# adaLN attention and gMLP block: first norm's modulation summed on TensorE, w_qkv read in column halves

## The chip, the cores and the metric

One core of one Trainium2 chip runs the kernel. The metric is the device time in microseconds of one execution, as the median of several runs. Five engines take part: TensorE (PE; its weight loads are PEld), VectorE (DVE), ScalarE (ACT), GpSimd (POOL) and SyncE (SP), which issues nearly all DMAs.

## The reference

All data is float32, S = 2048 rows, D = 448 columns, 16 heads of 28.

```python
x = A_x
mod = (silu(c) @ w_mod).reshape(1, 6, 1, 448)
sa, ca, ga, sb, cb, gb = mod[:, 0], ..., mod[:, 5]
h = layernorm(x) * (1 + ca) + sa
q, k, v = split(h @ wqkv)                 # 448 -> 3 x 448, 16 heads of 28
o = softmax(q @ k.T * 28**-0.5) @ v
x = x + ga * (o @ wo)
h = layernorm(x) * (1 + cb) + sb
z = gelu(h @ w_in)                        # 448 -> 1792
g = w_sp @ layernorm(z[..., 896:]) + b_sp # mixes the 2048 rows
x = x + gb * ((z[..., :896] * g) @ w_out)
```

## The kernel before

The stages come one after the other: projections of the first norm (about the first 95 us, with the rest of q and k up to 165 us), attention head by head, the output projection, the gMLP's two input projections, the row mixing and the output. The change is in the projections.

**Numbers.** A product keeps float32 accuracy by splitting each factor into a rounded high part and the remaining low part (`hi`, `lo`; `sub` computes `lo = value - hi`, line 83) and adding up the products. `STEPS` lists the 11 pairs (part of hT, part of the weight) that make one product over the 448 rows of a weight; 448 is three chunks of 128 and one of 64, and the low part of the last chunk lies in the upper half of its tile. So one V tile (128 rows of x, `v_tiles`, line 271) and one q/k unit (128 columns of w_qkv by 512 rows, `qk_unit(m, g)`, line 280) are 11 matmuls each. The columns of q and k are seven blocks m = 0 to 6; head 0 needs blocks 0 and 3.

**Groups.** The 2048 rows of x are four groups g of four tiles. For each group: `load_x`; `ln_stats` (VectorE's statistics, then `rstd_of`, two small POOL instructions, lines 106 and 107); `ln_norm` (VectorE's four `xn` tiles, line 253; POOL copies the last 64 columns once more behind them, line 263); `ln_transpose` (TensorE's 16 transposes into four PSUM tiles, line 116; then for chunks c = 0, 2, 1, 3 the scale and shift by the columns `ca` and `sa`, the rounding to hi, and lo). For groups 1 to 3 scale and rounding are ScalarE's (lines 123 and 130) and lo is POOL's. Group 0 shares them out between ScalarE with POOL and VectorE.

**Modulation.** `w_mod` is read in three pairs (sa with ca, ga with sb, cb with gb), each as four tiles of 112 rows. `mod_acc(pair, k)` adds `silu[k] * wm` on VectorE (lines 214 and 216). `mod_col` turns a summed row into per-partition columns by matmuls with ones (line 222); `mod_bc` broadcasts a row to all partitions by a matmul (line 230). Pair 0 is summed ahead of the first transposes' use, pair 1 at the end of group 1 and pair 2 at the end of group 2; `ga` and `sb` are made at the end of group 2's V tiles, `cb` and `gb` after group 3.

**Weights.** `load_w` reads w_qkv by row chunks: the V part (448 columns) and, into the same four buffers (tag `raw`), the q/k part of 896 columns. ScalarE makes the high parts (`wv_hi` line 297, `weight_part` line 94); POOL makes V's low parts, and POOL and VectorE alternate for q and k.

**Order.** The schedule is written by hand: every engine executes its instructions in the order in which the program issues them, and so does SP with its DMAs. PSUM has a ring of seven tiles (`bank`) and one more (`ps_o`). In each group the order on TensorE is: V tiles, the next group's transposes, the other V tiles, q/k units 0 and 3. `pe_fill` runs matmuls whose result nobody reads. After group 3, units (m, g) for m = 4, 1, 5, 2, 6 and all g follow; between their steps `m_first` computes the first 80 score products for the row maxima (line 399), each followed by a reduction on VectorE (line 404). They read q and k of the first heads, which go through DRAM (`qk_scr`, line 288) and come back by `load_head`.

Of the kernel before, what the change touches and what calls it, by code (L numbers as in the profile page):

```python
# [8 lines left out]
F32 = mybir.dt.float32  # L9
# [24 lines left out]
def tile_adaln_mha_gmlp(ctx, tc, x, wqkv, wo, w_in, w_spT, b_sp, w_out, cT, w_mod, out):  # L34
# [47 lines left out]
    def sub(eng, dst, a, hi):  # L82
        eng.tensor_tensor(out=dst, in0=a, in1=hi.bitcast(F32), op=ALU.subtract)  # L83
# [2 lines left out]
        eng.dma_start(dst[0:64], src)  # L86
        eng.dma_start(dst[64:128], src)

    def weight_part(dst, i, raw, hi_eng, lo_eng, zero=True):

        n = raw.shape[-1]
        h = dst[:, i if i < 3 else 6, 0:n]
        if hi_eng is act:
            act.activation(h, raw, AF.Copy)
        else:
            hi_eng.tensor_copy(h, raw)
        if i < 3:
            sub(lo_eng, dst[:, 3 + i, 0:n], raw, h)
        else:
            sub(lo_eng, dst[0:64, 7, 0:n], raw[0:64], h[0:64])  # L100
            if zero:
                pool.memset(dst[64:128, 7, 0:n].bitcast(F32), 0.0)

    def rstd_of(var, rs, n):

# [55 lines left out]
    def bank(name):  # L161
        return ring.tile([128, 512], F32, name=name, tag="s")

    def load_mod(pair, eng):
        for k in range(4):
            wms[pair, k] = e1.tile([112, 2, D], F32, name="wm", bufs=4)
            eng.dma_start(wms[pair, k], w_mod[:, pair, k])

    def load_x(g, eng):
# [3 lines left out]
        for t in range(4):  # L173
            xts[4 * g + t] = xg[:, t, :]

    def load_w(kind, i, eng):
        c0, n = (2 * D, D) if kind == "v" else (0, 2 * D)
        raw = e1.tile([128, 2 * D], F32, name="raw", bufs=4)[:, :n]
# [4 lines left out]
        raws[kind, i] = raw  # L183

    cc_t = e1.tile([112, 4], F32, name="cc_t", bufs=1)
    sp.dma_start(cc_t, cT)
# [13 lines left out]

    wu = bank("wu")

    def pe_fill(n):
        for _ in range(n):
            pe.matmul(wu[:, 0:128], ones, ones, start=True, stop=True)

    accs = {}

# [6 lines left out]
        else:  # L215
            dve.scalar_tensor_tensor(out=acc, in0=wm, scalar=silu[:, k : k + 1], in1=acc, op0=ALU.mult, op1=ALU.add)

    def mod_col(*parts):
        pc = bank("pc")
        for i, (nm, acc, plus1) in enumerate(parts):  # L220
            for c, r, e in ((0, 0, 128), (1, 0, 128), (2, 0, 128), (3, 0, 64), (3, 64, 128)):
                pe.matmul(
                    pc[r:e, 4 * i + c : 4 * i + c + 1], acc[:, c * 128 : c * 128 + e - r], ones[:112, 0:1], start=True, stop=True
                )
        for i, (nm, acc, plus1) in enumerate(parts):
            dve.tensor_scalar(out=cols[nm], in0=pc[:, 4 * i : 4 * i + 4], scalar1=plus1, scalar2=None, op0=ALU.add)

    def mod_bc(nm, acc):
        pc = bank("pc")
# [18 lines left out]
    def ln_norm(g):  # L248
        mv, rs = mv1.pop(g)
        res = []  # L250
        for t in range(4):
            xn = e1.tile([128, 512], F32, name="xn", bufs=4)
            dve.tensor_scalar(
                out=xn[:, :D],
                in0=xts.pop(4 * g + t),
                scalar1=mv[:, t, 0:1],
                scalar2=rs[:, t : t + 1],
                op0=ALU.subtract,
                op1=ALU.mult,
            )  # L260
# [5 lines left out]
    def v_tiles(*kts):  # L266
        pvs = [bank("pv") for _ in kts]
        for j, (a, b) in enumerate(STEPS):
            for kt, pv in zip(kts, pvs):
                g, t = divmod(kt, 4)  # L270
                pe.matmul(pv[:, :D], hT[g][:, a, t * 128 : (t + 1) * 128], wv[:, b, :], start=j == 0, stop=j == NST - 1)  # L271
        for kt, pv in zip(kts, pvs):
            dve.tensor_copy(V[:, kt, :, 0:DH], pv[:, :D].rearrange("p (h d) -> p h d", d=DH))

    def qk_unit(m, g, mid=None):
        pq = bank("pq")
        for j, (a, b) in enumerate(STEPS):
            if mid and j in mid:
                mid[j]()
            pe.matmul(pq, wqk[:, b, m * 128 : (m + 1) * 128], hT[g][:, a, :], start=j == 0, stop=j == NST - 1)  # L280
        f = stage.tile([128, 512], F32, name="qf")
        act.activation(f, pq, AF.Copy)  # L282
        hi = stage.tile([128, 512], F32R, name="qh")
        act.activation(hi, f, AF.Copy)
        lo = stage2.tile([128, 512], F32R, name="ql")
        sub(pool, lo, f, hi)
        for i, t in enumerate((hi, lo)):
            sp.dma_start(qk_scr[i][m * 128 : (m + 1) * 128, g * 512 : (g + 1) * 512], t.bitcast(F32))

    ln_stats(0)  # L290
    mod_acc(0, 0)
    mod_acc(0, 1)
    xns = ln_norm(0)
    mod_acc(0, 2)
    mod_acc(0, 3)
    def wv_hi(i):
        act.activation(wv[:, i if i < 3 else 6, :], raws["v", i], AF.Copy)

    def wv_lo(i):
# [3 lines left out]
        else:  # L303
            sub(pool, wv[0:64, 7, :], raw[0:64], wv[0:64, 6, :])

    for i in (0, 2):
        wv_hi(i)
        wv_lo(i)

    def wv_rest(c):  # L310
        if c == 2:
            wv_hi(1)
            wv_lo(1)
        if c == 1:
            wv_hi(3)
            wv_lo(3)

    def mod_first():
        pe_fill(4)
        mod_col(("ca", accs[0][:, 1, :], 1.0), ("sa", accs[0][:, 0, :], 0.0))  # L320
        pe_fill(10)

    ln_transpose(
        xns, e1, hT[0], cols["ca"], cols["sa"], (act, act, dve, dve), (pool, pool, dve, dve), mod_first, wv_rest
    )
    load_x(1, sp)
    for i in range(4):
        load_w("qk", i, sp)
    ln_stats(1)
    xns = ln_norm(1)  # L330
    for g in range(NG):
        if g + 2 < NG:
            load_x(g + 2, sp)
        if g in (0, 2):
            load_mod(1 + g // 2, sp)
        if g == 3:
            early.close()
            stk = att.enter_context(tc.tile_pool(name="stk", bufs=1))
            kq = [[stk.tile([128, S], F32R, name=f"{n}st{i}") for n in "kq"] for i in range(3)]
            kst, qst = [a[0] for a in kq], [a[1] for a in kq]  # L340
            npool = att.enter_context(tc.tile_pool(name="npool", bufs=2))

            def load_head(h, c0=0, c1=S):
                k, q = kst[h % 3], qst[h % 3]
                if h < 2 and c0 == 0:
                    pool.memset(k[64:86, :].bitcast(F32), 1.0)
                for r0, i in ((0, 0), (56, 1), (28, 0)):
                    sp.dma_start(k[r0 : r0 + 28, c0:c1].bitcast(F32), qk_scr[i][D + h * DH : D + (h + 1) * DH, c0:c1])
                for r0, i in ((0, 0), (28, 1), (56, 0)):
                    sp.dma_start(q[r0 : r0 + 28, c0:c1].bitcast(F32), qk_scr[i][h * DH : (h + 1) * DH, c0:c1])  # L350

            load_head(0, 0, 1536)
            for m in (0, 3):
                qk_unit(m, g)
            load_head(0, 1536, S)
        if g == 0:
            v_tiles(0, 1)
            v_tiles(2)
        else:
            v_tiles(4 * g)  # L360
            v_tiles(4 * g + 1)
        if g == 0:
            for i in range(4):
                weight_part(wqk, i, raws.pop(("qk", i)), act, (dve, pool)[i % 2], False)
        if g + 1 < NG:
            ln_transpose(xns, e1, hT[g + 1], cols["ca"], cols["sa"], (act,) * 4)
        if g + 2 < NG:
            ln_stats(g + 2)
            xns = ln_norm(g + 2)
        if g > 0:  # L370
            v_tiles(4 * g + 2)
        else:
            pool.memset(V[:, :, :, DH:32], 1.0)
        v_tiles(4 * g + 3)
        if g == 2:
            mod_bc("ga", accs[1][:, 0, :])
            mod_col(("sb", accs[1][:, 1, :], 0.0))
        if g < 3:
            for m in (0, 3):
                qk_unit(m, g)  # L380
        if g in (1, 2):
            for k in range(4):
                mod_acc(g, k)
    mod_col(("cb", accs[2][:, 0, :], 1.0))
    mod_bc("gb", accs[2][:, 1, :])
    late_e.close()

# [577 lines left out]
```

## Time and profile before

| | |
|---|---|
| median of 3 runs | 1462.51 us (lowest 1462.17, one run of 3635.17) |
| profiled execution | 1460.85 us, its span 1459.1 us |
| PE busy, PEld | 1436.4 us (98%), 1017.5 us |
| DVE, ACT, POOL busy | 881.3, 732.4, 276.3 us |
| granted TensorE clock, mean over the span | 0.997 |
| first matmul | 13.14 us after the span's start |
| first V matmul | 22.38 us |
| unit (0, 0): three matmuls, then a wait | 35.08 us, goes on at 38.87 us |
| first score matmul | 95.2 us |

The span is the time from the first to the last instruction of the profiled execution. A chain row gives start, length and the work that the end of the run depended on. A row of windows gives, for a stretch of time, the busy time and number of instructions of each engine, the granted TensorE clock, the DMA engines' busy share and GB/s. A row of groups gives line, engine, operation, output and inputs, shape and count; behind the bar the busy time and the mean ns of one, and then the idle time of the engine just before them.

### The profile page before, as it was taken

What the parts mean: (1) busy time and instruction counts of PE and PEld (TensorE: products, weight loads), DVE (VectorE), ACT (ScalarE), POOL (GpSimd) and SP (SyncE); (2) the same over time, 40 slices, a digit from 0 to 9 for tenths busy, and PEclk for the clock granted to TensorE, in tenths of its full rate; (3) what the DMA queues carried; (4) which work ended last, traced back from release to release, by engine and by line L of the source; (5) the groups of instructions that cost most, each with busy time, mean ns of one, the idle gap of its engine ahead of it and who ended that gap; (6) DMA issues with size and microseconds to landing.
All of it is one profiled execution on the core that took longest, in us unless ns stands there. A gap on an engine that the chain in (4) does not pass through costs nothing.

```text
span 1459.1 us, 19621 instructions
## 1 busy us (share of the span) xinstructions
PE 1436.4 (98%) x7314; PEld 1017.5 (70%) x7314; DVE 881.3 (60%) x1458; ACT 732.4 (50%) x1390; POOL 276.3 (19%) x255
## 2 busy tenths in 40 slices
PE   6999999999999999999999999999999999999999
PEld 5887755555555555555555556888988888888887
DVE  6557888888888888888888832921542411414114
ACT  3523576777677767777776786452432211211111
POOL 6734200000002021001000022100663400302002
PEclk9999999999999999999999999999999999999999
DMA  7564401221022211222132003432003322323223
GB/s 216 149 173 152 139 11 43 53 51 42 15 52 53 53 38 42 53 51 53 32 76 53 10 19 124 155 120 94 14 23 97 121 76 67 108 64 100 84 69 108
DMA packets 56131, 111.23 MB, mean 76 GB/s; under 512 B 11900, under 2 KB 22780, under 8 KB 53516
## 3 DMA queue, kind: packets, MB, share of 16 engines
q1 hardware_dynamic: 55910, 109.81, 25.9%
q8 instruction: 57, 0.93, 0.3%
q14 instruction: 38, 0.31, 0.1%
q10 hardware_dynamic: 126, 0.17, 0.0%
HBM read 75.89 MB, written 29.48 MB: 72 GB/s over the span
## 4 chain that ended last, share of the span: by engine, by line
PE 94%; DVE 3%; DMA 2%; issue 1%; SPq 0%; ACT 0%; POOL 0%; DVEq 0%; ACTq 0%
PE st_ps L430 18%; PE mt L399 16%; PE o_ps L445 16%; PE acc L848 6%; PE acc L850 6%; PE acc L849 6%; PE pq L280 5%; PE z_ps L802 5%; PE z_ps L736 5%; PE pv L271 2%; PE y_ps L889 2%; PE y_ps L888 2%; PE y_ps L890 2%; PE tp L116 1%; PE wo_ps L618 1%
## 5 line engine op out<-in xcount | busy, mean ns | idle before, releaser
L404 DVE TENSOR_REDUCE pm<-mt 128x1 f32<-128x512 f32 x1024 | 632.3, 683 | 120.6 <-PE mt L399 120.2
L434 ACT ACTIVATE P<-st_ps 128x512 f32<-128x512 f32 x1024 | 514.4, 621 | 153.4 <-PE st_ps L430 153.0
L430 PE MATMUL st_ps<-qst,kst 86*128 86x512 f32 x1024 | 410.6, 412 | 0.0
L399 PE MATMUL mt<-kst,qst 84*128 84x512 f32 x1024 | 405.7, 396 | 0.3 <-DVE pm L404 0.3
L430 PEld LDWEIGHTS st_ps<-qst,kst 86*128 86x128 f32 x1024 | 193.1, 189 | 145.2 <-issue 82.1
L445 PE MATMUL o_ps<-P,V 128*32 128x512 f32 x2048 | 247.5, 599 | 0.0
L399 PEld LDWEIGHTS mt<-kst,qst 84*128 84x128 f32 x1024 | 195.1, 190 | 37.1 <-DVE pm L404 0.7
L83 DVE TENSOR_TENSOR wsp_l<-raw_sp,wsp_h 128x512 fp32r<-128x512 f32 x64 | 50.8, 796 | 189.4 <-ACT wsp_h L785 189.4
L785 ACT ACTIVATE wsp_h<-raw_sp 128x512 fp32r<-128x512 f32 x64 | 40.2, 631 | 232.1 <-DMA raw_sp<-in_w_spT_dram 191.1
L445 PEld LDWEIGHTS o_ps<-P,V 128*32 128x32 f32 x2048 | 54.2, 109 | 123.4 <-issue 116.1
L83 POOL TENSOR_TENSOR heapF<-u,heapD 128x512 fp32r<-128x512 f32 x27 | 44.6, 1684 | 256.8 <-ACT heapD L867 256.8
L848 PE MATMUL acc<-wsp_h,heapD 128*128 128x512 f32 x224 | 87.7, 392 | 1.3 <-DVE u L865 1.3
L850 PE MATMUL acc<-wsp_h,heapD 128*128 128x512 f32 x224 | 87.5, 390 | 0.0
L849 PE MATMUL acc<-wsp_l,heapD 128*128 128x512 f32 x224 | 87.4, 390 | 0.0
L471 POOL TENSOR_TENSOR osb<-osb,rb 128x512 f32<-128x512 f32 x15 | 19.2, 1277 | 355.3 <-DMA rb<-r_scr 263.8
L280 PE MATMUL pq<-heapD 128*128 128x512 f32 x196 | 64.6, 407 | 0.0
L83 POOL TENSOR_TENSOR nl<-nf,nh 16x128 fp32r<-16x128 f32 x16 | 7.2, 449 | 278.9 <-issue 147.5
L893 DVE TENSOR_TENSOR x2t<-x2t,y_ps 128x448 f32<-128x448 f32 x12 | 7.4, 621 | 72.9 <-PE y_ps L890 72.9
L282 ACT ACTIVATE qf<-pq 128x512 f32<-128x512 f32 x28 | 16.7, 597 | 69.0 <-PE pq L280 69.0
L848 PEld LDWEIGHTS acc<-wsp_h,heapD 128*128 128x128 f32 x224 | 42.1, 188 | 10.5 <-DVE u L865 2.3
L850 PEld LDWEIGHTS acc<-wsp_h,heapD 128*128 128x128 f32 x224 | 42.1, 188 | 8.9
L849 PEld LDWEIGHTS acc<-wsp_l,heapD 128*128 128x128 f32 x224 | 42.1, 188 | 8.2
(162 smaller groups left out, 1753.8 us busy)
## 6 DMA issues: line engine op xcount, KB each, us to landing
raw_sp<-in_w_spT_dram SPq DMA_DIRECT2D x64, 256.0 KB
kst<-qk_scr SPq DMA_DIRECT2D x45, 224.0 KB
qst<-qk_scr SPq DMA_DIRECT2D x45, 224.0 KB
qk_scr<-qh SPq DMA_DIRECT2D x28, 256.0 KB
qk_scr<-ql SPq DMA_DIRECT2D x28, 256.0 KB
z_scr<-z1t SPq DMA_DIRECT2D x28, 256.0 KB
z<-z_scr SPq DMA_DIRECT2D x28, 256.0 KB
wm<-in_w_mod_dram SPq DMA_DIRECT2D x12, 392.0 KB
```

What stands on the lines that cost most here:

```text
L83: eng.tensor_tensor(out=dst, in0=a, in1=hi.bitcast(F32), op=ALU.subtract)
L280: pe.matmul(pq, wqk[:, b, m * 128 : (m + 1) * 128], hT[g][:, a, :], start=j == 0, stop=j == NST - 1)
L399: pe.matmul(mt, qst[h % 3][0:84, t * 128 : (t + 1) * 128], kst[h % 3][0:84, kb * 512 : (kb + 1) * 512], start=True, stop=True)
L404: dve.tensor_reduce(out=pms[h][:, t, kb : kb + 1], in_=mt, axis=AX.X, op=ALU.max)
L430: pe.matmul(st, kst[h % 3][0:86, kt * 128 : (kt + 1) * 128], qst[h % 3][0:86, qb * 512 : (qb + 1) * 512], start=True, stop=True)
L434: act.activation(p, st, AF.Exp, scale=SCALE)
L445: pe.matmul(otile[h][32 * qb : 32 * qb + 32, :], V[:, kt, h, :], ptiles.pop((u, qb)), start=kt == 0, stop=kt == NT - 1)
L736: pe.matmul(ps_t, w1[:, b, f * 128 : (f + 1) * 128], h2T[g][:, a, :], start=j == 0, stop=j == NST - 1)
L802: pe.matmul(ps_t[:, :D], h2T[g][:, a, tt * 128 : (tt + 1) * 128], w2[:, b, hf * D : (hf + 1) * D], start=j == 0, stop=j == NST - 1)
L848: pe.matmul(acc[f], z2[st][:, 0, fs], hi, start=st == 0, stop=False)
L849: pe.matmul(acc[f], z2[st][:, 0, fs], lo, start=False, stop=False)
L850: pe.matmul(acc[f], z2[st][:, 1, fs], hi, start=False, stop=st == NT - 1)
```

## The change

- **Pair 0 on TensorE.** VectorE's `mod_acc(0, k)` and the first `mod_col` go. `sel` holds silu spread so that a matmul of a 128-column piece of `wm` with four columns of `sel` adds to one column of a PSUM tile and zero to its neighbours. `mod_sum(k)` accumulates the four tiles k in three PSUM tiles (`pcs`: chunks 0 and 2, chunk 1, chunk 3), `mod_cols` adds the 1 of `1 + ca` and writes the columns.
- **Group 0 in an order of its own.** The transposes stand tile by tile between the sums. VectorE makes the float32 value (`h_full`) from PSUM, ScalarE the rounded one (`h_hi`) from the same PSUM tile; lo is POOL's for chunk 0 and VectorE's for the others. Fills run from the time that tiles of x arrive. The four V tiles of group 0 go step by step together (`v_mm`), in an order of steps of their own.
- **w_qkv by columns.** Columns 0 to 511 (part "a", tag `wm`) and 512 to 895 (part "b", tag `raw`) are read and prepared apart, "a" ahead of group 0's units and "b" after them. Pair 1 of w_mod uses tag `wm`, pair 2 tag `raw`. POOL makes one of the eight low parts, VectorE seven.
- **Statistics a group ahead.** `ln_stats(2)` runs in group 0 and `ln_stats(3)` in group 1. VectorE writes the xn tails itself (ScalarE for group 0). Group 1's low parts move from POOL to VectorE.
- **Units.** Units 1 and 2 of group 0 move from after group 3 to group 0, around group 1's transposes. The first eight of the 18 later units have five score products between their steps, the others four as before.
- **Sums spread.** The sums of pairs 1 and 2 stand between V tiles and units of groups 1 and 2; `ga` and `sb` are made at the end of group 1.

The diff, cut to its core:

```diff
     def load_mod(pair, eng):
         for k in range(4):
-            wms[pair, k] = e1.tile([112, 2, D], F32, name="wm", bufs=4)
+            wms[pair, k] = e1.tile([112, 2, D], F32, name="wm", tag=("wm", "wm", "raw")[pair], bufs=4)
...
+    PARTS = {"v": (2 * D, D, "raw"), "a": (0, 512, "wm"), "b": (512, 384, "raw")}
...
+    load_x(1, sp)
...
     def ln_norm(g):
...
+            for o, i in ((xn[:, :D], xt), (xn[:, D:], xt[:, 384:D]))[: 1 if g == 0 else 2]:
+                dve.tensor_scalar(
+                    out=o, in0=i, scalar1=mv[:, t, 0:1], scalar2=rs[:, t : t + 1], op0=ALU.subtract, op1=ALU.mult
+                )
+            if g == 0:
+                act.activation(xn[:, D:], xn[:, 384:D], AF.Copy)
-        for xn in res:
-            pool.tensor_copy(xn[:, D:], xn[:, 384:D])
...
-    ln_stats(0)
-    mod_acc(0, 0)
-    mod_acc(0, 1)
-    xns = ln_norm(0)
-    mod_acc(0, 2)
-    mod_acc(0, 3)
...
+    sel = e1.tile([112, 4, 16], F32, name="sel", bufs=1)
+    dve.memset(sel, 0.0)
+    dve.tensor_copy(sel[:, :, 0:16:5], silu.rearrange("p (k o) -> p k o", o=1).broadcast_to([112, 4, 4]))
+    pcs = [bank("pc"), bank("pc"), ps_o.tile([128, 512], F32, name="pc", tag="o")]
+
+    def mod_sum(k):
+        wm = wms.pop((0, k))
+        for pc, cs, rows in ((pcs[0], (0, 2), (0,)), (pcs[1], (1,), (0,)), (pcs[2], (3,), (0, 64))):
+            for r0 in rows:
+                todo = [(part, c) for part in (1, 0) for c in cs]
+                for j, (part, c) in enumerate(todo):
+                    w = wm[:, part, c * 128 : min(D, (c + 1) * 128)]
+                    pe.matmul(
+                        pc[r0 : r0 + w.shape[-1], 0:4],
+                        w,
+                        sel[:, k, 4 * j : 4 * j + 4],
+                        start=k == 0 and j == 0,
+                        stop=k == 3 and j == len(todo) - 1,
+                    )
...
+    ln_stats(0)
+    pe_fill(8, xts[1])
+    pe_fill(4, xts[3])
+    xns = ln_norm(0)
...
+    mod_sum(0)
+    mod_sum(1)
+    tp_first(0)
+    tp_first(1)
+    mod_sum(2)
+    tp_first(2)
+    tp_first(3)
+    mod_sum(3)
+    pe_fill(3)
+    for i in (0, 2, 1, 3):
+        load_w("a", i, sp)
     for i in (0, 2):
         wv_hi(i)
         wv_lo(i)
...
+    mod_cols(0)
+    h_full(0)
+    h_hi(0)
+    h_full(2)
+    h_hi(2)
+    mod_cols(1)
+    mod_cols(2)
+    h_full(1)
+    wv_hi(1)
+    h_hi(1)
+    h_lo(0, pool)
+    wv_lo(1)
+    h_full(3)
+    wv_hi(3)
+    h_hi(3)
+    h_lo(2, dve)
+    h_lo(1, dve)
+    wv_lo(3)
+    h_lo(3, dve)
+    for i in (0, 2, 1, 3):
+        load_w("b", i, sp)
+    load_x(2, sp)
+    pvs = v_mm((0, 1, 2), [STEPS[j] for j in (0, 1, 2, 6, 3, 4, 7, 5, 8, 9, 10)], 3)
     ln_stats(1)
+    for i, eng in ((0, pool), (2, dve), (1, dve), (3, dve)):
+        qk_part("a", i, eng)
+    load_mod(1, sp)
+    v_copy(*pvs[0])
+    v_copy(*pvs[1])
     xns = ln_norm(1)
+    v_copy(*pvs[2])
+    v_copy(*pvs[3])
+    ln_stats(2)
+    qk_unit((0, 3), 0)
+    ln_transpose(xns, e1, hT[1], cols["ca"], cols["sa"], (act,) * 4, (dve,) * 4)
+    load_x(3, sp)
+    xns = ln_norm(2)
+    qk_unit((1,), 0)
+    qk_unit((2,), 0)
+    for i in (0, 2, 1, 3):
+        qk_part("b", i, dve)
+    load_mod(2, sp)
+    pool.memset(V[:, :, :, DH:32], 1.0)
+    for g in range(1, NG):
...
+        v_tile(4 * g)
+        if g == 1:
+            ln_stats(3)
+        v_tile(4 * g + 1)
         if g + 1 < NG:
             ln_transpose(xns, e1, hT[g + 1], cols["ca"], cols["sa"], (act,) * 4)
...
+        if g == 1:
+            xns = ln_norm(3)
+        for k in range(2):
+            v_tile(4 * g + 2 + k)
+            if g < 3:
+                mod_acc(g, k)
...
         if g < 3:
+            for k, m in enumerate((0, 3)):
+                mod_acc(g, 2 + k)
+                qk_unit((m,), g)
+            if g == 1:
+                mod_bc("ga", accs[1][:, 0, :])
+                mod_col((("sb", accs[1][:, 1, :], 0.0),))()
...
-    for i, (m, g) in enumerate((m, g) for m in (4, 1, 5, 2, 6) for g in range(NG)):
+    units = [(m, g) for m in (4, 1, 5, 2, 6) for g in range(NG) if g > 0 or m not in (1, 2)]
+    for i, (m, g) in enumerate(units):
...
-        qk_unit(m, g, {j: m_first for j in (1, 4, 7, 10)})
+        qk_unit((m,), g, {j: m_first for j in ((1, 3, 5, 7, 9) if i < 8 else (1, 4, 7, 10))})
```

More of the change, by code (lines that the diff above doesn't have):

```diff
@@ L87, in load_z, with weight_part @@
         eng.dma_start(dst[64:128], src)
-    def weight_part(dst, i, raw, hi_eng, lo_eng, zero=True):
-        n = raw.shape[-1]
-        h = dst[:, i if i < 3 else 6, 0:n]
+    def weight_part(dst, i, raw, hi_eng, lo_eng, zero=True, c0=0):
+        cs = slice(c0, c0 + raw.shape[-1])
+        h = dst[:, i if i < 3 else 6, cs]
         if hi_eng is act:
@@ L97, in weight_part @@
         if i < 3:
[L98 removed]
+            sub(lo_eng, dst[:, 3 + i, cs], raw, h)
         else:
[L100 removed]
+            sub(lo_eng, dst[0:64, 7, cs], raw[0:64], h[0:64])
             if zero:
[L102 removed]
+                pool.memset(dst[64:128, 7, cs].bitcast(F32), 0.0)
     def rstd_of(var, rs, n):
@@ L174, in load_x @@
             xts[4 * g + t] = xg[:, t, :]
+    PARTS = {"v": (2 * D, D, "raw"), "a": (0, 512, "wm"), "b": (512, 384, "raw")}
     def load_w(kind, i, eng):
-        c0, n = (2 * D, D) if kind == "v" else (0, 2 * D)
-        raw = e1.tile([128, 2 * D], F32, name="raw", bufs=4)[:, :n]
+        c0, n, tag = PARTS[kind]
+        raw = e1.tile([128, 2 * D], F32, name="raw", tag=tag, bufs=4)[:, :n]
         if i < 3:
@@ L201, in tile_adaln_mha_gmlp, with pe_fill @@
     wu = bank("wu")
-    def pe_fill(n):
+    def pe_fill(n, with_=None):
         for _ in range(n):
-            pe.matmul(wu[:, 0:128], ones, ones, start=True, stop=True)
+            pe.matmul(wu[:, 0:128], ones if with_ is None else with_[:, 0:128], ones, start=True, stop=True)
     accs = {}
@@ L216, in mod_acc, with mod_col, finish @@
             dve.scalar_tensor_tensor(out=acc, in0=wm, scalar=silu[:, k : k + 1], in1=acc, op0=ALU.mult, op1=ALU.add)
-    def mod_col(*parts):
+    def mod_col(parts, cs=(0, 1, 2, 3)):
         pc = bank("pc")
+        n = len(cs)
         for i, (nm, acc, plus1) in enumerate(parts):
-            for c, r, e in ((0, 0, 128), (1, 0, 128), (2, 0, 128), (3, 0, 64), (3, 64, 128)):
-                pe.matmul(
-                    pc[r:e, 4 * i + c : 4 * i + c + 1], acc[:, c * 128 : c * 128 + e - r], ones[:112, 0:1], start=True, stop=True
-                )
-        for i, (nm, acc, plus1) in enumerate(parts):
-            dve.tensor_scalar(out=cols[nm], in0=pc[:, 4 * i : 4 * i + 4], scalar1=plus1, scalar2=None, op0=ALU.add)
+            for j, c in enumerate(cs):
+                for r, e in ((0, 128),) if c < 3 else ((0, 64), (64, 128)):
+                    pe.matmul(
+                        pc[r:e, n * i + j : n * i + j + 1], acc[:, c * 128 : c * 128 + e - r], ones[:112, 0:1], start=True, stop=True
+                    )
+        def finish():
+            step = cs[1] - cs[0]
+            for i, (nm, acc, plus1) in enumerate(parts):
+                dve.tensor_scalar(
+                    out=cols[nm][:, cs[0] : cs[-1] + 1 : step],
+                    in0=pc[:, n * i : n * i + n],
+                    scalar1=plus1,
+                    scalar2=None,
+                    op0=ALU.add,
+                )
+        return finish
     def mod_bc(nm, acc):
@@ L252, in ln_norm, with v_mm @@
             xn = e1.tile([128, 512], F32, name="xn", bufs=4)
[L253 to L260, printed above, removed]
+            xt = xts.pop(4 * g + t)
+            for o, i in ((xn[:, :D], xt), (xn[:, D:], xt[:, 384:D]))[: 1 if g == 0 else 2]:
+                dve.tensor_scalar(
+                    out=o, in0=i, scalar1=mv[:, t, 0:1], scalar2=rs[:, t : t + 1], op0=ALU.subtract, op1=ALU.mult
+                )
+            if g == 0:
+                act.activation(xn[:, D:], xn[:, 384:D], AF.Copy)
             res.append(xn)
-        for xn in res:
-            pool.tensor_copy(xn[:, D:], xn[:, 384:D])
         return res
-    def v_tiles(*kts):
+    def v_mm(kts, steps=STEPS, last=None):
         pvs = [bank("pv") for _ in kts]
-        for j, (a, b) in enumerate(STEPS):
+        if last is not None:
+            kts, pvs = kts + (last,), pvs + [ps_o.tile([128, 512], F32, name="pv", tag="o")]
+        for j, (a, b) in enumerate(steps):
             for kt, pv in zip(kts, pvs):
@@ L279, in qk_unit @@
                 mid[j]()
[L280 to L288, printed above, removed]
-    ln_stats(0)
-    mod_acc(0, 0)
-    mod_acc(0, 1)
-    xns = ln_norm(0)
-    mod_acc(0, 2)
-    mod_acc(0, 3)
+            for m, pq in zip(ms, pqs):
+                pe.matmul(pq, wqk[:, b, m * 128 : (m + 1) * 128], hT[g][:, a, :], start=j == 0, stop=j == NST - 1)
+        for m, pq in zip(ms, pqs):
+            f = stage.tile([128, 512], F32, name="qf")
+            act.activation(f, pq, AF.Copy)
+            hi = stage.tile([128, 512], F32R, name="qh")
+            act.activation(hi, f, AF.Copy)
+            lo = stage2.tile([128, 512], F32R, name="ql")
+            sub(pool, lo, f, hi)
+            for i, t in enumerate((hi, lo)):
+                sp.dma_start(qk_scr[i][m * 128 : (m + 1) * 128, g * 512 : (g + 1) * 512], t.bitcast(F32))
     def wv_hi(i):
@@ L304, in wv_lo, with mod_cols, tp_first @@
             sub(pool, wv[0:64, 7, :], raw[0:64], wv[0:64, 6, :])
+    sel = e1.tile([112, 4, 16], F32, name="sel", bufs=1)
[9 more added lines that the diff above has]
+                    w = wm[:, part, c * 128 : min(D, (c + 1) * 128)]
+                    pe.matmul(
+                        pc[r0 : r0 + w.shape[-1], 0:4],
[3 more added lines that the diff above has]
+                        stop=k == 3 and j == len(todo) - 1,
+                    )
+    def mod_cols(b):
+        cs = ((0, 2), (1,), (3,))[b]
+        n = len(cs)
+        for i, (nm, plus1) in enumerate((("ca", 1.0), ("sa", 0.0))):
+            dve.tensor_scalar(
+                out=cols[nm][:, cs[0] : cs[-1] + 1 : 2], in0=pcs[b][:, n * i : n * i + n], scalar1=plus1, scalar2=None, op0=ALU.add
+            )
+    def tp_first(t):
+        for c in range(4):
+            pe.transpose(tps[c][:, t * 128 : (t + 1) * 128], xns[t][:, c * 128 : (c + 1) * 128], ident)
+    ln_stats(0)
+    pe_fill(8, xts[1])
+    pe_fill(4, xts[3])
+    xns = ln_norm(0)
+    tps, fs = {}, {}
+    for c in (0, 2, 1, 3):
+        tps[c] = bank("tp")
+    mod_sum(0)
[9 more added lines that the diff above has]
+        load_w("a", i, sp)
     for i in (0, 2):
@@ L308, in tile_adaln_mha_gmlp @@
         wv_lo(i)
[L310 to L328, printed above, removed]
@@ L329, in tile_adaln_mha_gmlp, with h_full @@
-    ln_stats(1)
-    xns = ln_norm(1)
[L331 to L335, printed above, removed]
+    def h_full(c):
+        if c in (0, 2):
+            fs[c] = e1.tile([128, 512], F32, name="hfull")
+        else:
+            fs[c] = stage.tile([128, 512], F32, name="hfull", tag="qf")
+        dve.tensor_scalar(
+            out=fs[c], in0=tps[c], scalar1=cols["ca"][:, c : c + 1], scalar2=cols["sa"][:, c : c + 1], op0=ALU.mult, op1=ALU.add
+        )
@@ new lines, in h_hi, with h_lo @@
+    def h_hi(c):
+        act.activation(
+            hT[0][:, c if c < 3 else 6, :], tps[c], AF.Identity, scale=cols["ca"][:, c : c + 1], bias=cols["sa"][:, c : c + 1]
+        )
+    def h_lo(c, eng):
+        if c < 3:
+            sub(eng, hT[0][:, 3 + c, :], fs[c], hT[0][:, c, :])
+        else:
+            sub(eng, hT[0][64:128, 6, :], fs[3][64:128], hT[0][64:128, 6, :])
+    mod_cols(0)
[6 more added lines that the diff above has]
+    h_full(1)
```

42 lines of the change are left out of this document (11 added, 31 removed).

## The prediction

> **What bounds the kernel now.** I read the header of the page first.
>
> ```profile
> span 1459.1 us, 19621 instructions
> PE 1436.4 (98%) x7314; PEld 1017.5 (70%) x7314; DVE 881.3 (60%) x1458; ACT 732.4 (50%) x1390; POOL 276.3 (19%) x255
> ```
>
> TensorE works for all of the span but 22.7 us. Then the chain of work that ended last, over the first 76 us (start, length, what):
>
> ```profile
> 3.07 8.34 DMA wm<-in_w_mod_dram
> 11.51 1.15 DVE acc L216
> ...
> 13.14 4.30 PE tp L116 x16
> 17.44 1.00 PE wu L205 x8
> 18.45 1.77 PE pc L222 x20
> 20.25 0.16 DVE col_ca L226
> ...
> 34.69 4.14 DVE heapF L83
> 38.87 7.40 PE pq L280 x19
> 46.27 4.48 PE pv L271 x22
> 50.75 1.75 PE tp L116 x16
> ```
>
> Up to 38.87 us the chain jumps between DMA, VectorE and TensorE; from there it is TensorE alone. So the change, which touches only the projections, can gain only before that point, plus what the restart cost: 19 matmuls took 7.40 us, while 22 of the same take 5.01 at 56.99. The windows say why (us, PE, PEld, DVE, ACT, POOL busy, then granted clock):
>
> ```profile
> 36.00:38.00 2.00, 0.00 (x0) 0.00 (x0) 2.00 (x1) 0.50 (x2) 2.00 (x3) 1.00 1.04 251
> 38.00:39.00 1.00, 0.13 (x1) 0.13 (x1) 1.00 (x2) 0.97 (x2) 1.00 (x1) 0.52 1.00 244
> 39.00:42.00 3.00, 3.00 (x7) 2.38 (x8) 2.21 (x8) 1.75 (x3) 2.63 (x3) 0.50 0.32 80
> 45.00:46.00 1.00, 1.00 (x6) 0.82 (x5) 1.00 (x3) 0.00 (x0) 1.00 (x3) 1.00 0.53 197
> ```
>
> TensorE stood still from 35.9 to 38.87 for a weight's low part on VectorE; about 2.1 us into that gap the granted clock fell to 0.50 and stayed there until about 45. Last, what VectorE pays (line, mean ns near the end), shapes kept apart, first 46 us:
>
> ```profile
> L83 DVE TENSOR_TENSOR heapF<-raw,heapD 128x896 fp32r<-128x896 f32 x1 | 4.2, 4200 | 0.0
> L83 DVE TENSOR_TENSOR heapD<-raw,heapD 128x896 fp32r<-128x896 f32 x1 | 1.9, 1884 | 0.0
> L83 DVE TENSOR_TENSOR heapD<-hfull,heapD 64x512 fp32r<-64x512 f32 x1 | 1.5, 1527 | 0.0
> L83 DVE TENSOR_TENSOR heapD<-hfull,heapD 128x512 fp32r<-128x512 f32 x1 | 0.7, 693 | 0.0
> ```
>
> One subtraction costs 0.69 us or several times that; the dear ones ran while POOL was full of its own subtractions. And the modulation sums, from VectorE's timeline:
>
> ```profile
> 62.71 1.07 DVE L214 TENSOR_SCALAR acc<-wm,silu 112x896 f32<-112x896 f32 x1
> 63.82 4.44 DVE L216 SCALAR_TENSOR_TENSOR acc<-wm,silu,acc 112x896 f32<-112x896 f32 x3
> 75.10 3.52 DVE L216 SCALAR_TENSOR_TENSOR acc<-wm,silu,acc 112x896 f32<-112x896 f32 x3
> ```
>
> **Part 1: the first norm's modulation on TensorE.** Removed from VectorE: one 0.69 us product and three of 1.15. They hold the first xn from 11.47 (rs ready) to 12.6, so the transposes can begin 1.1 us earlier. Added to TensorE: per w_mod part 20 instructions (10 float32 matmuls, two passes each) of the same weight widths as the 20 of the row "pc L222 x20", 1.77 us; four parts 7.1 us. The first part lands at 9.88 (VectorE's first sum starts there). From then TensorE has 7.1 us of sums and 16 transposes at 1.75: full until 18.7. The first accumulator (columns 0 and 2) closes after 8 instructions of the last part, 17.65. Two column adds (0.24), then ScalarE's 0.78 and VectorE's 0.82 from the same PSUM tile side by side: hi part 0 at 18.7. After the three fills TensorE starts on V at 19.45, against 22.38: 2.9 us earlier. The extra fills run from 4.7 to 9.9 us, when TensorE is idle: nothing. Without that cover they would cost 30 x 0.12 = 3.6 us. The xn tails go to ScalarE; no such row exists, between its 112x4 (0.21) and its 128x448 (0.57), I take 0.25; four end by 13.6, under the sums.
>
> **Part 2: V of group 0.** 44 matmuls at 4.48/22 = 0.204 us: 9.0 us, to 28.4. Each step serves four tiles (0.82 us). By ScalarE's order (wv 0.57, hi 0.78) hi 1 is ready at 21.1 and step four wants it at 21.9; the other parts have over 1 us of room. No stall, where before the 33 first matmuls were strung out over 8.4 us and the last 11 came behind the transposes.
>
> **Part 3: first four column blocks of w_qkv.** The halves of 512 columns take the w_mod buffers, so SP issues them once TensorE has finished each sum (11.7 to 18.7) and not when POOL is through with wv (17.9 to 28). At some 260 GB/s in the rows before, they land by about 24, ahead of ScalarE (0.6 each, 22.5 to 24.9). The low part that decides is block 0 on POOL: queued on VectorE ahead of it are three h low parts (to 24.8 at 0.69 to 1.53 each, middle) and the statistics of group 1 (2.48: the chain's 25.55 to 28.03), then POOL's rstd (1.45, to the first xn at 29.5) and the subtraction (1.34): 30.1. TensorE wants it at 28.4 + 4 x 0.233 = 29.3. A stall of 0.8 (bounds 0 and 2.3).
>
> **Part 4: to the end of group 1.** TensorE: units (0,3) 22 matmuls at 0.70 us per three (the chain's rows from 95.6 on), 5.13, to 34.3; transposes 1.75 (xn of group 1 is there at 33.6); the two moved units 5.13, to 41.2; two V tiles 4.48 with 0.2 lost to the last low part; transposes, two V tiles, two units: 57.2. VectorE is late meanwhile: four low parts paced by ScalarE (1.41 per block behind 2.46 of evictions) until 43.2; norm of group 2 2.3 (four rows of 0.44 apart, and four of 64 columns, some 0.12 each); four 384-column low parts that end after ScalarE's last hi, 47.9; V copy 0.6, statistics of group 3 2.48, V copy 0.6, rstd 0.9 beyond the copy, norm 2.3, V copy 0.6, then the sums of pair 1 with a V copy between: 0.69 + 3.45 at the quiet price, 1.07 + 4.44 at the price beside POOL, middle 4.9. End 60.7.
>
> **The new wait.** The broadcast of ga and the column of sb move from group 2 to the end of group 1, and TensorE's queue holds all of group 2 behind them. TensorE is there at 57.2, the sums at 60.7: it stands 3.5 us. In the trace before, the same sums ended at 68.3 and were wanted at 72.7.
>
> **The sum.** At 60.7 TensorE has done what before was done at 62.00 (end of group 1's units) plus two units, 5.13: 67.1. So 6.4 us ahead. The idle 3.5 us then costs clock. Before, 2.95 us idle cost 6 us at half clock, 3.0 us; between 1.7 and 3.4 by where the drop falls, I take 2.9. Net 3.5 us. Everything behind runs at the same TensorE work. The profiled execution took 1460.85 (span 1459.1 and 1.75 around it), so 1457.35 by it; the median of the runs shown is 1462.51, 1.7 higher, and on that scale I say 1459.0. The first eight later units carry five score matmuls each and not four: 16 x 0.233 = 3.74 us per unit on TensorE against 5 x 0.70 of reductions on VectorE, so nothing, and two units fewer make up the count.
>
> [...]
>
> **Rivals.**
> - *Short wait.* Subtractions and sums at the quiet price: the a parts 2.1 rather than 2.9, the b parts 0.5 less, the sums 4.1: 58.9. Then 1.7 us of idle, under the 2.1 that the drop took: 67.1 - 58.9 = 8.2, 1454.3; with no wait at all 9.9, 1452.6. For it: POOL loses most of its low parts. Against: its rows for group 2 fall just where the sums run.
> [...]
> - *Slower: VectorE pays the dear price.* By 4.20 us per 896 columns the three a parts cost 2.4 each (7.2, 4.3 more) and the four b parts 1.8 each (7.2, 4.8 more): the sums end at 69.8, later than the 67.1 of before, and 3.0 of half clock follow: 1462.5 + 2.7 + 3.0 = 1468.2. It decides from 3.5 us of extra on. For it: that row, and three more subtractions on VectorE per stage. Against: POOL then has one or two of its own beside them, not a full queue. [...]
> - *Five scores per unit bind on VectorE.* If each reduction takes 0.69 plus the 0.24 wait seen at 97.5, 4.65 per unit instead of 3.74: 8 x 0.9 = 7.3 us, 1466. Against: two of them back to back took 1.40.
>
> **How the numbers follow.** Forecast 0.40, short or no wait 0.25, full clock 0.12, dear price 0.13, five scores 0.05, something else 0.05. The range takes the short wait and most of the slower cases in: 1451.5 to 1466; the forecast's own is 1456.5 to 1462. A measurement of this kernel tells about 2% (29 us) from no change; no case reaches that. TensorE had by 46.27 done 17.6 us of work at full clock (32 transposes 3.5, 44 V matmuls 9.0, 22 of units 5.1), so the whole start is 28.7 us, so faster by 2% would need all of it and is almost out: 0.005. Slower by 2% needs a disturbance that I do not see: 0.025.
>
> **What would show it.** Right: V starts near 19.5, sums on TensorE without gaps from 9.9; no idle second longer than 1 us before 57; a TensorE wait on acc of some 3.5 us near 57 to 61 with a granted clock of 0.5 behind it; attention starting 3 to 4 us earlier. Wrong: no wait on acc, or a clock at 1.00 through it (then 1452 to 1456); DVE rows of L83 over 2 us, or pm waits in the first eight later units.

## The result and the profile after

The changed kernel takes 1471.36 us (median, 1470.15 to 1472.41), the kernel before 1462.34 beside it: ratio 1.0072, 95% interval 1.0056 to 1.0087. The ratio counts fast runs alone, so that it leaves out the run of 3635.17 us. The change is slower by 9.0 us between the medians and by 10.5 by the ratio, where the prediction said 3.5 us faster, with a range to 1466. The profiled execution took 1472.11 us, its span 1470.3. The page's header, with the clock's row of the 40 slices (tenths of full speed), and below it the same row of the kernel before:

```profile
span 1470.3 us, 19758 instructions
PE 1450.3 (99%) x7376; PEld 1031.2 (70%) x7376; DVE 892.9 (61%) x1482; ACT 733.3 (50%) x1398; POOL 259.7 (18%) x233
PEclk7989999999999999999999999999999999999999
```

```profile
PEclk9999999999999999999999999999999999999999
```

TensorE is busy for 13.9 us longer although it has only 62 more instructions, and the clock's row begins 7 9 8 where it was all nines: TensorE works slowly in places. The chain of work, first 95 us:

```profile
10.39 5.00 PE pc L342 x40
15.38 1.90 PE tp L360 x8
17.29 2.89 PE pc L342 x20
...
26.54 10.26 PE pv L291 x44
...
53.92 2.06 DVE xn L276 x4
...
74.51 1.16 DVE acc L223
75.72 1.86 PE pc L251 x2
...
78.96 6.89 PE pv L291 x22
85.85 1.75 PE tp L116 x16
```

V starts at 26.5 in the chain, at 26.2 in TensorE's timeline, where the kernel before has 22.4. A modulation sum (x20) takes 2.89 us, and 22 V matmuls behind the broadcast take 6.89 where 4.48 is their time. The windows show both stretches (granted clock behind POOL's column):

```profile
17.00:20.00 3.00, 3.00 (x22) 2.98 (x20) 0.00 (x0) 0.00 (x0) 1.38 (x2) 0.50 0.70 263
56.00:60.00 4.00, 4.00 (x19) 3.81 (x19) 4.00 (x9) 2.71 (x4) 0.00 (x0) 0.57 0.66 174
69.00:73.00 4.00, 0.00 (x0) 0.00 (x0) 4.00 (x5) 0.84 (x2) 2.02 (x2) 1.00 0.66 193
76.00:84.00 8.00, 8.00 (x26) 6.62 (x27) 1.39 (x3) 0.00 (x0) 0.00 (x0) 0.51 0.01 2
```

From 17 to 20 us TensorE has no idle moment and still gets half the clock. By the trace's record of the clock it was halved from 12.1 to 29.2, from 56.5 to 59.9 and from 73.5 to 83.8. In the row from 69 TensorE does nothing for 4 us while VectorE is full. What VectorE does there (its timeline: start, length), and the wait at the broadcast:

```profile
50.66 5.33 DVE L276 TENSOR_SCALAR xn<-xg,mv,rs 128x448 f32<-128x448 f32 x8
62.25 7.57 DVE L276 TENSOR_SCALAR xn<-xg,mv,rs 128x448 f32<-128x448 f32 x8 [0.96 <-POOL rs L107]
72.15 3.51 DVE L223 SCALAR_TENSOR_TENSOR acc<-wm,silu,acc 112x896 f32<-112x896 f32 x3
```

```profile
PE pc L251 <- DVE acc L223: 7.1, 1, 7.1
```

The norm of a group, the same eight instructions, took 2.67 us for group 1, 5.33 for group 2 and 7.57 for group 3. The predicted wait is there, with twice its length.

### The profile page after: what moved, and what is told of

The parts are those of the page before. It is cut to its first block, busy times and chain, and to the rows that moved or that the text cites. A ratio compares the mean times of both kernels' runs of the same rounds, so it can differ in the third digit from the quotient of the medians.

```text
span 1470.3 us, 19758 instructions
## 1 busy us (share of the span) xinstructions
PE 1450.3 (99%) x7376; PEld 1031.2 (70%) x7376; DVE 892.9 (61%) x1482; ACT 733.3 (50%) x1398; POOL 259.7 (18%) x233
## 4 chain that ended last, share of the span: by engine, by line
PE 92%; DVE 3%; DMA 2%; issue 1%; ACT 1%; POOL 0%; SPq 0%; DVEq 0%; ACTq 0%; POOLq 0%
PE st_ps L533 18%; PE mt L502 16%; PE o_ps L548 16%; PE acc L952 6%; PE acc L954 6%; PE acc L953 6%; PE z_ps L906 5%; PE z_ps L840 5%; PE pq L306 4%; PE pv L291 2%; PE y_ps L993 2%; PE y_ps L992 2%; PE y_ps L994 2%; PE pc L342 1%; DMA raw_sp<-in_w_spT_dram 1%
```

## The experiments

Three theories: (a) the broadcast's wait on the sums, with the half clock behind it, makes the loss; (b) the sums on TensorE, with a moving operand of four columns, do not hold the clock, and so eat the start's gain; (c) VectorE is late because its instructions, the norms above all, are held up by POOL. The rivals stand with each run. All times stand beside the kernel before on the same chip; the changed kernel was timed only for the result above, so a difference from it also holds what the sessions differ by (the kernel before took 1460.85 to 1462.34).

**Late broadcast (a_bc_late).** For (a):

```diff
             v_tile(4 * g + 2 + k)
+            if g == 2 and k == 0:
+                mod_bc("ga", accs[1][:, 0, :])
+                mod_col((("sb", accs[1][:, 1, :], 0.0),))()
...
-            if g == 1:
-                mod_bc("ga", accs[1][:, 0, :])
-                mod_col((("sb", accs[1][:, 1, :], 0.0),))()
```

> The changed kernel, with the broadcast of ga and the column of sb behind the third V tile of group 2 instead of at the end of group 1; the sums themselves stay where they are. Theory (the wait on the sums and the half clock behind it are the loss): TensorE reaches the broadcast 3 V tiles and 16 transposes (8.5 us) after the end of group 1, so the wait of 7.1 us and the half clock of 73.5 to 83.8 us (4.0 us lost) go: 1471.4 - 11 = 1460. Rival (VectorE as a whole is late, and the next thing that it owes, the V copies that free PSUM, makes TensorE wait instead): less than half of it comes back, 1466 or more.

Measured 1459.84, ratio 0.9991 (0.9981 to 1.0000): 11.5 us less than the changed kernel. TensorE's timeline has no wait at that line any more, and the two instructions run at full clock:

```profile
78.45 0.92 PE L251 MATMUL pc<-acc,ones 112*128 112x448 f32 x2
```

The sums still ended at 77.3; they were only not needed yet. The slow start was still there, with V at 27.9: the first 40 sum instructions took 6.28 us (5.00 in the changed kernel). The windows show a clock of 1.00 for that stretch only because the record of the clock has its first entry at 30.5 us in this execution. So (a) holds, with the size expected: this one wait, with the half clock behind it, costs about as much as the whole loss.

**Wide sums (a_wide).** For (b): the same 80 instructions with 128 moving columns, all but one of them zero (of the four, all but one were zero too), kept in V's memory, which is not yet in use.

```diff
-    sel = e1.tile([112, 4, 16], F32, name="sel", bufs=1)
+    sel = V[0:112, :, 0:4, :].rearrange("p n a b -> p n (a b)")
...
-                        pc[r0 : r0 + w.shape[-1], 0:4],
+                        pc[r0 : r0 + w.shape[-1], 0:128],
                         w,
-                        sel[:, k, 4 * j : 4 * j + 4],
+                        sel[:, 4 * j + k, :],
```

> The changed kernel, with the moving operand of the modulation sums 128 columns wide instead of 4 (124 of them zero); same count of matmuls and weights. Theory (the clock monitor does not count matmuls of 4 columns as work, so the sums, the transposes between them and the first V steps run at half clock from 12.1 to 29.2 us): the clock stays at 1.0 from about 12 us on, a sum takes 1.8 us instead of 2.9, V starts near 20 instead of 26.5; VectorE's chain starts 5.5 us earlier as well, so 5 to 6.5 us come through: 1465.5. Rival (the clock falls for another reason, or VectorE's chain behind it is bound elsewhere): clock 0.5 as before, or a longer wait on the sums of pair 1 in its place, 1470 to 1472.

Measured 1465.97, ratio 1.0027 (1.0015 to 1.0038). TensorE's timeline and the window from 17 us:

```profile
15.24 2.10 PE L343 MATMUL pc<-V,wm 112*128 112x128 f32 x20
...
21.30 9.35 PE L291 MATMUL pv<-wv,heapD 128*128 128x448 f32 x44
```

```profile
17.00:20.00 3.00, 3.00 (x34) 2.71 (x30) 0.67 (x3) 0.00 (x0) 0.67 (x1) 1.00 0.96 363
```

More data through TensorE (128 columns for four), and each sum is a third shorter (x20: 1.93 us in the chain, against 2.89): the clock stays at 1.00 from 9.9 to 50.9, V starts 4.9 us earlier (21.3 against 26.2), and 5.4 us come through. The wait on the sums is 7.1 us here too: they end 5.1 us earlier (70.5 against 75.7), and TensorE comes 5.1 us earlier. So (b) holds. The other traces agree. In all eight with 32 columns or more the clock is at 1.00 from its first entry, at 8 to 11 us, to beyond 40 us. In the five with four columns it either falls 3.4 or 6.8 us after its first entry, while the sums run, or has none before 30 us (a_bc_late).

**Group 2's low parts on VectorE (a_lo_dve).** For (c): `los` of `ln_transpose` is `(dve,) * 4` for group 2.

> The changed kernel, with group 2's four low parts on VectorE instead of POOL, ahead of the norm of group 3 in VectorE's queue. Theory (the norm of group 3 took 7.6 us because POOL subtracted beside it; alone it takes 2.7): VectorE gets more work, four times 0.7 us, and is done sooner: low parts by 62, norm by 65, sums of pair 1 by 71 instead of 75.7; 4 to 5 us come back, and up to 4 more if the clock no longer falls: 1463 to 1467. Rival (the norm is slow for its eight instructions, not for POOL): the sums end 2.8 us later, 1474.

Measured 1469.82, ratio 1.0060 (1.0045 to 1.0076): 1.5 us less, not 4 to 8, and within the noise, since the two intervals overlap. The norm of group 3 fell from 7.6 to 4.7 us, not to 2.7, since two of POOL's subtractions for q and k still ran beside it, and it started 3.2 us later behind the low parts. The sums ended 0.4 us earlier and TensorE waited for them longer, 8.3 us. This run gives no answer by itself.

**All three (a_all), and the first two alone (a_bc_wide).**

> The three edits above together: wide sums, group 2's low parts on VectorE, late broadcast. Theory: both losses go and the start's gain comes through, the wait on the sums is covered: 1471.4 - 11 - 6 = 1454, 8 us ahead of the kernel before. Rival (VectorE's work is the bound in groups 0 and 1 whatever the order): 1460, no better than the late broadcast alone.

> The changed kernel with late broadcast and wide sums only; group 2's low parts stay on POOL. Theory (low parts on VectorE gave 1.5 us where a wait depended on them; with the broadcast late hardly anything does): the sums end some 0.5 us later than with all three edits and TensorE's wait on them is 1.3 to 2 us: 1455.5 to 1457. Rival (VectorE's relief from POOL counts in full): 1459.

Measured 1455.61, ratio 0.9962 (0.9947 to 0.9977), and 1455.14, ratio 0.9960 (0.9945 to 0.9975). Late broadcast and wide sums carry it all; where the low parts are computed no longer matters. Both still wait at the broadcast (1.3 and 1.5 us), by the trace for a V copy that stands right behind the sums in VectorE's queue, and have 3.4 us of half clock behind that.

**POOL's subtractions left out (c_nopool).** The test of (c): the changed kernel, VectorE's work untouched.

```diff
-            lo = stage2.tile([128, 512], F32R, name="ql")
-            sub(pool, lo, f, hi)
+            lo = hi
+            if g >= 2:
+                lo = stage2.tile([128, 512], F32R, name="ql")
+                sub(pool, lo, f, hi)
...
-            ln_transpose(xns, e1, hT[g + 1], cols["ca"], cols["sa"], (act,) * 4)
+            ln_transpose(xns, e1, hT[g + 1], cols["ca"], cols["sa"], (act,) * 4, (act if g == 1 else pool,) * 4)
```

> The changed kernel with POOL's subtractions left out around the two slow norms: for groups 0 and 1 the low parts of q and k are not computed (the high part is stored twice), and group 2's low parts are ScalarE copies of the value, for the fourth chunk nothing; VectorE's instructions are unchanged. It prices what POOL's company costs VectorE. Theory: both norms take 2.7 us and the sums 4.2; the sums of pair 1 end 8 us earlier, TensorE comes 2 to 3 us earlier and its wait falls from 7.1 to about 2: 1471.4 - 8 = 1463, and with no fall of the clock 1460. Rival (VectorE is slow for another reason, such as the DMAs that land then): norms as before, 1470.

Measured 1460.10, ratio 0.9995 (0.9985 to 1.0005). VectorE's timeline:

```profile
48.33 2.68 DVE L279 TENSOR_SCALAR xn<-xg,mv,rs 128x448 f32<-128x448 f32 x8
57.27 2.68 DVE L279 TENSOR_SCALAR xn<-xg,mv,rs 128x448 f32<-128x448 f32 x8 [0.97 <-POOL rs L107]
```

Both norms are back at 2.68 us, the wait at the broadcast is 2.5 instead of 7.1, and no matmul waits on an xn tile in group 2. The sums of pair 1 end 10.6 us earlier (65.0 against 75.7): 7.5 come from the norms, 0.7 from the first product of the sums (0.68 instead of 1.43), and 2.4 from the start, where the half clock is still there but shorter in this execution (14.4 to 28.0 us, V at 23.8). So (c) holds: POOL's company cost VectorE 2.7 and 4.9 us in the norms alone. Of the 11 us that the run gains, some 2 are the start's. This is what POOL did beside the norm of group 3 in the changed kernel, five subtractions:

```profile
62.19 2.71 POOL L83 TENSOR_TENSOR heapD<-hfull,heapD 128x512 fp32r<-128x512 f32 x2
65.05 3.12 POOL L83 TENSOR_TENSOR heapD<-hfull,heapD 128x512 fp32r<-128x512 f32 x2 [0.15 <-ACT heapD L130]
68.24 1.52 POOL L83 TENSOR_TENSOR ql<-qf,qh 128x512 fp32r<-128x512 f32 x1
```

**ScalarE writes the xn tails: on the changed kernel (c_tails), with all three edits (b_tails), and there with the broadcast behind the fourth V tile (b_best).** `ln_norm` issues four VectorE instructions instead of eight; `act.activation(xn[:, D:], xn[:, 384:D], AF.Copy)` in every group.

> The changed kernel with nothing but the 64-column copies of groups 1 to 3 on ScalarE. Theory (VectorE's instructions wait behind POOL's subtractions one by one): the norm of group 2 ends before POOL's subtractions start and takes 1.8 us instead of 5.3, the norm of group 3 about half of 7.6; but the POOL work that it met is then met by the sums behind it, which go from 4.9 to 6 or 7. The sums of pair 1 end 3 to 4 us earlier and so does all of it: 1467 to 1468.5. Rival (the cost goes by elements): 1470.5.

> All three edits, and the last 64 columns of xn copied by ScalarE in every group, so that VectorE's norm of a group is four instructions, not eight. Theory (beside POOL's subtractions each of VectorE's instructions waits its turn, whatever its width: the 64-column form took 0.79 us on average and the 448-column form 0.67): the norms of groups 2 and 3 take about half, 2.7 and 2.4 us instead of 5.3 and 4.7; TensorE's wait of 1.7 us before group 2's transposes and the 1.3 us on the sums go, and the half clock behind it (1.7): 1451.5. Rival (time goes by elements, so that the tails are an eighth): norms of 4.7 and 4.1, 1455.

> As the run with ScalarE's tails, and the broadcast of ga behind the fourth V tile of group 2 instead of the third, with the first sums of pair 2 behind it. Theory: if the tails alone take the wait away, the same time within 0.5 us, 1451.5; if they do not, this takes away what is left of the wait on the sums and of the half clock behind it (1.3 + 1.7): 1452.5. Rival (the wait only passes on to the sums of pair 2 or to the V copies): 1455.

Measured 1469.87 (ratio 1.0064, 1.0047 to 1.0081), 1457.29 (0.9970, 0.9956 to 0.9985) and 1453.21 (0.9944, 0.9930 to 0.9959). The first two are misses. On the changed kernel the norm of group 3 did not halve (c_tails first, then the sums of b_tails):

```profile
61.20 5.80 DVE L276 TENSOR_SCALAR xn<-xg,mv,rs 128x448 f32<-128x448 f32 x4 [0.97 <-POOL rs L107]
```

```profile
63.58 6.37 DVE L223 SCALAR_TENSOR_TENSOR acc<-wm,silu,acc 112x896 f32<-112x896 f32 x3
```

Four instructions in 5.80 us are 1.45 each, the length of one POOL subtraction (1.26 to 1.55 beside and behind this norm in the changed kernel). In the norm of group 3 of the changed kernel five of the eight instructions were long, as many as POOL had subtractions there: the first of 448 columns (1.49 us) and the four of 64 (1.28 on average). The other three took 0.50. So what counts is not how many instructions VectorE issues, which was the theory, but how many subtractions POOL has beside them. The norms of group 3 bear this out: beside five subtractions 4.89 us over the quiet 2.68, beside two 2.05 and 2.01 (a_all, a_lo_dve), beside one 0.98 (b_units), and with four instructions beside four subtractions 4.02 over the quiet 1.78 (c_tails). That is about 1 us for each. The norm of group 2 lost 2.65 beside two subtractions and a memset of V. In c_tails the sums ended 1.6 us earlier (74.0), TensorE came 5.2 us earlier, waited 10.7 us for them instead of 7.1, and the clock was at half from 65.3 to 82.4. That its time is near the rival's is luck: a cost by elements is not what the rows show.

In b_tails the norm of group 3 is quiet at 1.79 us and the three sums meet POOL instead: 6.37 where 3.5 is the quiet time. The delay was handed on; TensorE waited 2.4 us and the clock fell for 6.8. With the broadcast one V tile later (b_best) the wait is 0.6 us, the clock stays at 1.0 from 10.5 us on, and the kernel is the fastest of all, 8 us ahead of the one before.

**The moved units back (b_units).** All three edits, units 1 and 2 of group 0 after group 3 again, four scores everywhere.

> All three edits, but units 1 and 2 of group 0 back after group 3, with four scores in every unit. Theory (the moved units are cover: TensorE works on them for 5.1 us while ScalarE and VectorE prepare group 1): TensorE comes to group 1's V tiles 5 us earlier and waits there for the low parts, which depend on ScalarE; nothing is gained for the work moved out: 1455.6 + 4 to 5 = 1460, and with a fall of the clock 1462. Rival (VectorE and ScalarE run ahead as well, since two evictions fewer stand before them): 1456 to 1457.

Measured 1458.50, ratio 0.9977 (0.9968 to 0.9986): 2.9 us more than with the units moved by the medians, 2.2 by the ratios, whose intervals just overlap; between theory and rival. TensorE waits 1.8, 0.9 and 0.4 us in group 1's first V tile, and the clock is at half from 41.3 to 48.1. The moved units are cover worth 2 to 3 us.

**32 and 64 columns (b_w32, b_w64).**

> All three edits of the earlier run, but the modulation sums 32 columns wide, not 128. Theory (what counts is the share of time in which columns stream): 32 columns are 13 ns out of 88 per instruction, so the clock falls to 0.5 as with 4 columns, a sum takes 2.9 us: 1455.6 + 5 = 1460. Rival (any matmul counts whose operand is not tiny): clock at 1.0 and 1455.6.

> The same with 64 columns, 27 ns of 88, 30%. In the kernel before, a stretch of 3.4 us with 1.3 us of matmuls (38%) ended in a fall of the clock. Theory: 0.5 here too, 1460. Rival: 1.0 and 1455.6.

One run each: 1455.06 and 1454.43. The theory of the streaming share falls. Its 13 and 27 ns were the author's estimates; by the rows of the kernel before (22 matmuls of 512 columns in 5.01 us, 22 of 448 in 4.48) 64 columns are 24 ns and 32 are 12. The windows with 4 columns (the changed kernel) and with 32:

```profile
15.00:17.00 2.00, 2.00 (x16) 1.98 (x15) 0.00 (x0) 1.15 (x2) 0.85 (x1) 0.50 1.02 306
```

```profile
15.00:17.00 2.00, 2.00 (x24) 1.92 (x24) 0.00 (x0) 1.15 (x2) 1.20 (x2) 1.00 1.07 256
```

With 32 columns 40 instructions of the sums take 3.67 us and the clock holds; with four they took 3.58 where they ran at full clock (c_nopool). In these runs four columns did not hold it (0.50 in the window from 15) and 32 did (1.00); where between them the bound lies, and what is counted, stays open.

## Why the prediction was wrong

The new wait with half clock behind it was forecast, and the runs show it as the loss. What failed are two terms of the sum that set its length: the sums on TensorE (Part 1) and VectorE's norms (Part 4). VectorE's sums of pair 1 ended 15.0 us later than forecast: 6.0 of these were there when VectorE made its first columns (23.6 instead of 17.65), and 8.3 came in the two norms.

- **Right: the place of the new wait, the moved units and the five scores.** TensorE waits at the broadcast on the sums of pair 1, as forecast, with half clock behind it. The first units with five scores take 3.73 to 3.74 us each in the chain (3.74 forecast), without waits on `pm`. In the wide-sum run TensorE waits 0.9 us for block 0 of w_qkv on POOL, which was forecast as 0.8.
- **Part 1, the sums' price (7.1 us for four, V at 19.45).** Each was taken from the 1.77 us of 20 instructions before, at full clock. The first two measured 5.00 together, the others 2.89 each, the transposes beside them 1.90 instead of 0.88 per eight, and V's 44 matmuls ran slow as well (10.26 instead of 9.0): V started at 26.54. The old row stood between wide fills; in the change nothing wide runs beside the sums for 15 us but twice eight transposes. The forecast's sentence on the fills counted their time and not what they do for the clock. The wide-sum run prices this step at 5.4 us.
- **Part 4, "norm of group 2 2.3" and of group 3.** They measured 5.33 and 7.57; even a quiet one took 2.67. The dear-price rival had POOL's company as the cause and nearly the time (1468.2), but charged it to the subtractions, which have two inputs, at 1.8 and 2.4 us each. Those averaged 0.54 to 1.37 us by form in the changed kernel; the larger bill, 2.65 and 4.89 us in the two norms, came from instructions with one tensor input. So the nearness of its time is in part luck. The forecast's price was that of the norms before, 1.78 us for four instructions, which ran beside POOL's short copies.
- **The new wait, 3.5 us.** 7.14, at 68.6 to 75.7: VectorE came 15 us later than forecast (60.7 to 75.7), TensorE 11 (57.2 to 68.6).
- **Clock behind it, 2.9 us.** From 75.7 to 83.8 TensorE worked 8 us at half clock: 4.0 lost. The forecast's bounds, 1.7 and 3.4, are half of slow stretches of 3.41 and 6.83 us; this one lasted 10.24. For the chance of 0.12 on a full clock behind the wait no run shows a ground: the clock was at 0.51 in the window from 76. A second fall, 56.5 to 59.9, came behind waits of 1.4 and 0.3 us on xn tiles, and cost some 1.7; the forecast held waits under 2 us harmless. That one was a matter of luck, as the last section shows.
- **The sum.** When the sums were done, TensorE had the work behind it that the kernel before had done at 67.0 to 67.1: not 6.4 us ahead but 8.7 behind, and 12.8 behind after the half clock. The span is 11.2 longer: 12.0 us of the 12.8 are left when attention starts (its first row of st_ps at 177.6 against 165.6), 11.2 when it ends (first row of wo_ps at 904.6 against 893.4). Why was not followed up. As single repairs, the late broadcast brings 11.5 us and the wide sums 5.4; together 16.2.

POOL's company did not slow all of VectorE's work. A norm of eight instructions took 2.68 us without it and 5.33 and 7.57 beside POOL, the first product of the sums 0.68 and 1.43. The V copies out of PSUM took 0.58 to 0.62 us throughout, those at 36.2 and 69.7 beside a POOL subtraction too. Why the ones and not the others was not shown.

## What to carry to other kernels

Work given to TensorE for its spare time is worth its time only at the clock that it keeps itself: 20 instructions priced at 1.77 us took 2.89 at half clock here. Look at the granted clock around the row that you price it from, and pad narrow matmuls where that costs next to nothing (40 took 3.58 us with four columns, at full clock in c_nopool, and 3.67 with 32). Before a consumer is moved forward, price its producer's engine with its neighbours, instruction by instruction; here a slow neighbour's delay did not vanish when one instruction got out of its way, it met the next (a_all to b_tails: the norm of group 3 from 4.73 to 1.79 us, the three sums from 4.43 to 6.37). The two long waits on TensorE were paid twice: the 2.95 us of the kernel before cost 3.0 us of clock on top, the 7.1 us here 4.0. So first move the wait, then shorten the work.

## What was not expected of the hardware

- TensorE without an idle moment (3.00 of 3.00 us busy in the window from 17) got half the clock while it ran matmuls of four moving columns with some transposes between them (12.1 us to the first V matmuls, and with them to 29.2), and full clock with 32, 64 or 128 columns in the same order of instructions (1.00 in the windows from 15 to 20 us of b_w32, b_w64 and a_wide). So idle time does not explain this fall; what does was not shown. The slow stretches lasted 17.07, 3.41 and 10.24 us in the changed kernel, 6.83 in the kernel before and 13.65 in c_nopool, all multiples of 3.41.
- Waits of 1.4 and 0.3 us within 2.0 us were enough for 3.41 us of half clock (56.5 to 59.9), but not always. Eight traces have the same two waits. In four the clock fell (after, a_bc_late, a_wide, b_w64), in four it did not (a_lo_dve, a_all, a_bc_wide, b_w32). Counted in steps of 3.41 us from the edges of the clock's record, TensorE was busy for 1.73 to 1.75 us of the step with these waits where the clock fell behind it, and for 1.91 to 2.08 where it did not. So in these eight the fall went with the place of the waits in such a step.
- Beside POOL's subtractions a 64-column instruction of VectorE took longer than one of 448: in the norm of group 3 1.28 and 0.75 us on average, 0.31 and 0.51 without them.
